# FFN weight blocks W1 and W3 in transfers of 256 rows, with another order of the products

## Chip, core and metric

One NeuronCore of a Trainium2 chip runs the whole program. The metric is the device time of one execution in microseconds (us), the median of several. The engines are PE (TensorE: `MATMUL`, with its weight loads shown as PEld), DVE (VectorE), ACT (ScalarE), POOL (GpSimd) and SP (SyncE), which here only issues transfers.

## What is computed

Two layers with shared weights, each a recurrent attention over 64 segments of 32 tokens with 8 memory tokens, and then a gated FFN. `x` is 2048 x 576, there are 32 heads of 128, and the FFN is 4608 wide; all inputs are bf16.

```
def _A_ref(x, mem0, Wq, Wk, Wv, Wo, seg_len):
    mem = mem0
    for s in range(n_seg):
        h = concatenate([mem, x[segment s]])                 # 8 + 32 tokens
        q, k, v = h@Wq, h@Wk, h@Wv                           # 32 heads of 128
        p = softmax(where(mask, q k^T * scale, -1e9))
        o = (p v) @ Wo
        mem = o[:8];  outs.append(o[8:])
def _B_ref(x, w1, w3, w2):
    return (silu(x@w1) * (x@w3)) @ w2
x = x + A(layernorm(x));  x = x + B(layernorm(x))            # layer 0
x = x + A(layernorm(x));  x = x + B(layernorm(x))            # layer 1
```

The memory makes each segment wait for the one before it, so PE is filled with several things at once.

## The kernel before

**Tiling.** 72 steps are run: in step t layer 0 works on segment t and layer 1 on segment t - 8, so that for most steps 2 x 40 query columns go through PE together. Attention weights stay in SBUF (tiles W, WV, WO). The FFN runs once per four steps as a "job" over 128 tokens of each layer, in 18 pairs of 128 hidden columns. For each pair the weights are fetched anew from HBM: `load_w13` brings 576 rows x 256 columns of W1 and of W3 into one of two buffers of tile W13, and `load_w2` brings 256 x 576 of W2 into one of two buffers of tile W2C. All of these transfers are issued by SP, one behind the other, and each waits there until PE has read the old content of its place. One pair's loads are, before the change, two transfers of 512 rows (256 KB), two of the last 64 rows (32 KB, the "tails"), and one of 288 KB for W2. In the profile tile W13 appears as `W`, like the attention weights.

**Completion marks.** SP's transfers use eight semaphores in turn, so a transfer also waits, before it is issued, until the one eight places ahead of it has landed.

**The order of products.** `make_nodes` builds a graph of nodes: a node is a group of matmuls (some 1 to 2 us), an evacuation, a step of the softmax, or a load. `plan` (line 76) places them. PE's order isn't searched there: it is read from the strings FIRST, FOUR and LAST (lines 199 to 222), one letter per node, joined as `ORDER = FIRST + FOUR * 11 + LAST`. FIRST has 805 letters, FOUR 224 (four steps and one FFN job, run eleven times), LAST 684. The other engines' nodes are put by `plan` at the first place where their inputs, buffers and engine are free by its own cost figures, and the program is recorded in that order. The letters are:

```
Q, q  products for q and k (32 full matmuls; 8 of the last 64 rows)     S  scores     T  transpose of p
P     p v         O, o  output product (32; 8)                           V, v, X, x, G, g  products for v
F, f  FFN up (16 full; 4 of the last 64 rows)   W, w  FFN down of the two layers   n, p, a, b, m  transposes
```

The string decides how far a product stands behind the ones it depends on: S waits for the evacuated q and k of its group (QKT), T for the softmax (SME, STAT, PB), P for the evacuated transposes (PTS), O for the evacuated P (OT), W for HTT.

**Forms of a product.** A node may run on the whole 128 x 128 array ("full"), in two column halves ("col", which issues each matmul as two with 64 columns of weights), in two row halves ("row", for contractions over 64 rows), or in quarters. `settle` in `plan` lets a node that may be full or col keep the form of its neighbours, so the string also decides how many matmuls are issued and how often the form changes.

**Step 0.** Its two V products, for tokens (VX) and for memory (VM), are issued as one sequence by `v_run` (line 871) when the second of them comes up in the order, whichever that is.

The lines of the profile: L591 is every matmul and weight load, L594 every ACT instruction, L597 every DVE instruction, L600 every transfer that SP issues, L1010 the clearing of PB on POOL.

Of the kernel before, what the change touches and what calls it, by code (L numbers as in the profile page):

```python
# [13 lines left out]
P = 128  # L14
# [30 lines left out]
class Slot:  # L45


    def __init__(self, pool, users=1):
        self.pool, self.users, self.i, self.end, self.begun = pool, users, None, 0.0, False
# [144 lines left out]
def ewh(*ns):  # L194
# [2 lines left out]


FIRST = (
    "amqqQQQQqSQqqQqSqqQSQTSvxVXPTPTOPTOPooOOooQQqqqqQSQvqqSVQQqTqSQPQOSToPXTOPTxoPOOooQqqqQQSVvqQQSQqqqQSqTQPOSTPTOP"  # L200
    "OToooPaOoQQqqqqQQSvSVQqqqQQQSqTPSXTOPTOPoTxoPOOooQQpQqqqvVqSnQQSFfqFQqfqqQTQSPFTfSOFPWOToPFToffPOOooWQqqqqQQSQQS"
    "FFfqfVvqTQWQqSFxffqQFPSXTWfPFTOPOTOPFOooooWQfqqqQQSFqfqVvQQSFfqTQPWQSqqfFTQOSfoPFTOPWFTOPooffOoFQqqQqqvSQQWSVqqf"
    "FQQWqqSTQPQSTOPabOTXPooTOPxxOooXqqpQQQqqSQnVvfSFTQqqqQQPSFffqQFTOPoSWTFfPOOTFPWOooofQQqfqqFSQFqqfgQGWTQPQSfqFQQq"
    "fqFSWTGFSggfGPGTOPOTfgFaPOOooooWVvqqfQQFFQSqfqQWQSqqfFQTQQqfqSFPWTSFPOTfoOPFWTOPffFOoooWQQqqqqQSbQQQqgqSGSTGPQTq"
    "gqQPOggSGTGPOTOPoooOoQqqqpQVpSQnQvqqqQnQFSTffqFQQPqSwTFPSffOOWTFPFTOPWOoooowFffqqQQQWSfqqFQwQSFqfqgGTQQPWfqSTFFg"
    "gfqGQwPGTOoSPFgfOGTOPWOoooFqqfqQQQQvSwqVSFqqfQQWwTFPQfqfqFTQSwPWSfFOTFPWwOTffFPOOaooooWQQqqqqQwSbQGQgqqSQTQPQqqg"
    "SGTSGPGggTOPOTOPoooOo"
)
FOUR = (
    "QvqqpQQpQqqVSSnnQQFqfqfFQTQfqqWSFPwTFPSfOOTFPwTOPWOooooFffqqQQQQqqSWFSFffqgGQTQPQQgqqqGSwTFPGSfgfgFTGOPOWTOPwOoo"  # L210
    "ooFqqQQQQqfqVvSSwWFfqfqQQTFWQwQSFffqqFPWTOPSowTFPffOTOFPWwOoooFqqfqQQQWQSqqqaQSQQbQqgqSGTSGPgTGPOTggOPGTOPwOoooo"
)
LAST = (
    "QqqqpQQQSnpQQqqqVSvTSnQFffqPFOQqTwPoSWTFPffFTOOWPwOoooFFqfqQQQqqfSQQwQfqqFTSGSqfgQFPWQgfqGTSFPGFTfggOOPGTOPwWOoo"
    "ooFFqffqQQwQWQSqqVSvqqQQTFQPSfqqQwTOWSPFTFPofOTOPwOoooWFfqfqQQQQqfqSFwWvVSFTfqqQQPWQqqSvTQVSPOTbOPwOTooPoxOoXqQp"
    "pVvQqqqQSQQnqqSQnqQFTSfqQPFTSOPfTFOPwTOPWOooooFqfqfQQQSVqqqvQQQwSfqFWTFPSfqqQTQOPSFTwfFPOTOPWOooooFfqqQQQSqfxvVX"
    "qfFQwWTSQFQqqqfQPWSTwFPffqQFTWSOwFPffOFTOPwOooooWFvqfqQQQSWqqVQwSFfqqfQFTQQSqqWPQTPSOoTOPwOToobPxOoXqqqQQQpvSVqQ"
    "qQSnqQFfSTQFPqqfQOTSFfPwTOoofPFTOPFOfoowQqqQFSQfqqqQQSVvqqfQFTQFSfqPQOTowPSFTfxXPOTOPFOooowVvqqQQQSqqfQQSqqfQFST"
    "QQPwqqFTSOfPFTOfPwTOPfoooOoFQQqqqqQSQQSqqQVvSfTFPqQQwqfTSFPOTOFPTOPfoooOoFpwnfffFFwFwfffFFFwfffFFwFwfffFFFwfffFF"
    "wFwfffFFFfww"  # L220
)
ORDER = FIRST + FOUR * 11 + LAST
# [2 lines left out]
class Opt:  # L225

    qk, qkt, sc, tr, pv, wo, wog, vm = 0.0079, -0.0342, 0.0268, 0.1447, 0.0406, 0.2653, 0.0725, 0.1407
    vmt, vx, vxt, ff, fft, win, w2, gstep = -0.0231, 0.2313, 0.0843, 0.2124, -0.1839, 0.8 * (LAG - 4), 0.1943, 0.0624
    ustep, mode_pen, hor, wait, bulk, ff_split, last_win, tail_at = 0.0315, 0.1194, 0.0162, 0.141, 0.02, False, 2.5, -1.5

# [337 lines left out]
class Emitter:  # L568


    def __init__(self, nc, tc, T, aps, nseg):
        self.nc, self.tc, self.T, self.nseg = nc, tc, T, nseg
        self.a = aps
        self.last = {}
        self.order_dep = mybir.DependencyInfo(mybir.DependencyClass.NoSync, mybir.DependencyReason.SCHED_ONLY)
        self.tail_w, self.ys, self.mode, self.v0 = {}, {}, None, []


    def ch(self, eng, inst):
# [111 lines left out]
    def load_w13(self, pr, w13):  # L691
        def f(n):
            fa = pr * 2 * P
            W = self.T.W13[:, w13.i]
            for kind, wd in ((0, self.a.w1), (1, self.a.w3)):
                self.dma(W[:, 4 * kind:4 * kind + 4], wd[0:4 * P, fa:fa + 2 * P].rearrange("(c p) f -> p c f", p=P))
            for kind, wd in ((0, self.a.w1), (1, self.a.w3)):
                self.dma(W[kind * R64:(kind + 1) * R64, 8], wd[4 * P:D, fa:fa + 2 * P])
        return f
# [168 lines left out]

        return [(p0, m, row, 2 * q + r) for p0, _, q, m, row in strips]

    def v_run(self, t, b, strips, tail):

        if t or tail:
            self.v_mm(t, [(b, strips)], tail)
            return
        self.v0.append((b, strips))
        if len(self.v0) == 2:
            self.v_mm(t, self.v0, False)

    def vx(self, t, k, b, tail):  # L880
        return lambda n: self.v_run(t, b, self.vx_strips(t, k), tail)

    def vm(self, t, k, b, tail):
        return lambda n: self.v_run(t, b, self.vm_strips(t, k), tail)

    def v_ev(self, b, p0, width, row, blk):
        return lambda n: self.cp(n, self.T.V[row:row + width, blk, :], self.bk(b)[p0:p0 + width, :])
# [444 lines left out]
```

## Time and profile before

| | us |
|---|---|
| median of 3 runs | 2688.06 (2684.2 to 2690.27) |
| profiled execution, its own time | 2690.27 |
| its span, first to last instruction | 2688.5 |
| PE busy in the span | 2621.6 |
| DVE busy | 2113.0 |
| ACT busy | 1346.6 |
| SP waiting for PE before an issue, in total | 1849.0 |

PE is busy for 98% of the span. Busy time of PE is a union of overlapping matmuls, so it is the time in which PE always had at least one product under way. The granted clock is 0.995. The transfers move 322.08 MB, 478177 packets, at a mean of 120 GB/s.

### The profile page before, as it was taken

The page shows a single profiled execution, that of the slowest core. Times are in us where ns is not written, and L with a number is a line of the kernel's source. Part 1 is how long each engine was busy: PE and PEld are TensorE (multiplying, and loading weights), DVE is VectorE, ACT ScalarE, POOL GpSimd, SP SyncE. Part 2 cuts the span into 40 slices and gives each one's busy share as a digit, 9 for nine tenths or more (in the row PEclk, how much of TensorE's full clock was granted, in tenths as well). Part 3 has the DMA queues.
Part 4 walks back from the last instruction along what each step waited for, and adds up shares of the span by engine and source line. Part 5 has one row for each costly group of instructions (what it writes and reads, how often), then busy time and mean ns, then how long its engine had stood idle before and what let it go on. Part 6 is the DMA issues. An engine that isn't in the chain of part 4 may idle for free.

```text
span 2688.5 us, 136826 instructions
## 1 busy us (share of the span) xinstructions
PE 2621.6 (98%) x60872; PEld 2292.9 (85%) x60925; DVE 2113.0 (79%) x5486; ACT 1346.6 (50%) x3915; POOL 332.2 (12%) x400
## 2 busy tenths in 40 slices
PE   5999999999999999999999999999999999999998
PEld 4788888889888888988888888888888888888886
DVE  4788887887878778788877878787787878787876
ACT  2655554454545455454545445454544545554552
POOL 1111110110111011011101101110110111011110
PEclk9999999999999999999999999999999999999999
DMA  9064524344343334434233443424343342334467
GB/s 318 4 180 124 159 76 125 89 120 118 102 124 88 111 98 119 118 107 126 82 112 96 119 118 108 128 78 115 93 123 114 109 134 73 116 91 134 129 175 239
DMA packets 478177, 322.08 MB, mean 120 GB/s; under 512 B 26024, under 2 KB 467760, under 8 KB 476944
## 3 DMA queue, kind: packets, MB, share of 16 engines
q1 hardware_dynamic: 474048, 305.43, 38.7%
q8 instruction: 477, 7.82, 1.2%
q0 software_dynamic: 3024, 6.93, 0.9%
q10 hardware_dynamic: 512, 0.94, 0.2%
q14 instruction: 116, 0.95, 0.1%
HBM read 308.49 MB, written 2.36 MB: 116 GB/s over the span
## 4 chain that ended last, share of the span: by engine, by line
PE 90%; DVE 3%; DMA 3%; ACT 2%; issue 1%; SPq 1%; POOL 0%; ACTq 0%; DVEq 0%; POOLq 0%
PE bank L591 90%; ACT V L594 1%; DMA W<-in_B_w_dram 1%; SPq L600 1%; DMA W<-in_A_Wk_dram 1%; DVE V L597 1%; DVE STAT L597 1%; DVE SME L597 1%; DMA XN<-in_A_x_dram 0%; ACT SME L594 0%; DVE PTS L597 0%; DVE PB L597 0%; ACT PTS L594 0%; DVE HTT L597 0%; DMA W2C<-in_B_w_dram 0%
## 5 line engine op out<-in xcount | busy, mean ns | idle before, releaser
L591 PEld LDWEIGHTS <-W 128*128 128x128 bf16 (+2 forms) x32064 | 1267.6, 100 | 124.9 <-issue 60.0
L591 PE MATMUL bank<-HT,W 128*128 128x80 bf16 (+3 forms) x23040 | 807.6, 197 | 18.7 <-issue 5.8
L591 PE MATMUL bank<-XTB,W 128*64 128x256 bf16 (+5 forms) x9024 | 664.4, 263 | 6.3 <-DMA W<-in_B_w_dram 3.7
L594 ACT ACTIVATE QKT<-bank 128x256 bf16<-128x256 f32 (+2 forms) x1477 | 343.6, 314 | 365.5 <-PE bank L591 337.5
L1010 POOL MEMSET PB<- 128x1024 bf16 x288 | 273.9, 951 | 1888.2 <-PE bank L591 1531.3
L591 PE MATMUL bank<-OT,WO 128*128 128x80 bf16 (+3 forms) x11520 | 409.7, 198 | 4.9 <-issue 3.4
L591 PEld LDWEIGHTS <-WO 128*128 128x128 bf16 (+1 forms) x11520 | 380.7, 102 | 30.4 <-issue 18.4
L594 ACT ACTIVATE V<-bank 32x512 bf16<-32x512 f32 (+1 forms) x594 | 335.8, 585 | 110.7 <-PE bank L591 104.4
L591 PE MATMUL bank<-WV,HT 128*32 128x512 bf16 (+4 forms) x3628 | 366.8, 384 | 4.5 <-issue 2.2
L591 PE MATMUL bank<-W2C,HTT 128*64 128x288 bf16 (+1 forms) x3040 | 320.5, 287 | 2.1 <-DMA W2C<-in_B_w_dram 1.4
L597 DVE TENSOR_REDUCE STAT<-SME 104x8 f32<-104x320 f32 (+1 forms) x576 | 274.5, 477 | 17.7 <-ACT SME L594 11.9
L597 DVE TENSOR_TENSOR PB<-SME,STAT 40x128 bf16<-40x128 f32 (+4 forms) x912 | 275.5, 336 | 10.8
L594 ACT ACTIVATE HTT<-bank 128x512 bf16<-128x512 f32 (+1 forms) x324 | 177.6, 557 | 200.4 <-PE bank L591 199.1
L591 PEld LDWEIGHTS <-HT 128*32 128x32 bf16 (+4 forms) x3680 | 158.0, 100 | 119.6 <-issue 17.7
L591 PEld LDWEIGHTS <-HTT 128*64 128x64 bf16 (+1 forms) x3104 | 229.9, 104 | 34.0 <-issue 2.1
L597 DVE SCALAR_TENSOR_TENSOR XR<-bank,XR 128x288 f32<-128x288 f32 x576 | 239.6, 446 | 17.2 <-PE bank L591 14.5
L597 DVE CAST QKT<-bank 128x128 bf16<-128x128 f32 (+4 forms) x571 | 154.6, 316 | 124.6 <-PE bank L591 123.5
L597 DVE SCALAR_TENSOR_TENSOR HTT<-HTT,bank 128x512 bf16<-128x512 bf16 (+1 forms) x324 | 202.0, 623 | 56.6 <-ACT HTT L594 52.4
L594 ACT ACTIVATE OT<-bank 128x320 bf16<-128x320 f32 (+1 forms) x425 | 157.0, 405 | 168.9 <-PE bank L591 165.1
L597 DVE TENSOR_TENSOR HTT<-HTT,bank 128x512 bf16<-128x512 bf16 (+1 forms) x324 | 203.5, 628 | 28.3 <-PE bank L591 0.5
L594 ACT ACTIVATE PTS<-bank 128x320 bf16<-128x320 f32 (+1 forms) x394 | 148.1, 405 | 131.6 <-PE bank L591 93.7
L594 ACT ACTIVATE SME<-SME 104x320 f32<-104x320 f32 (+1 forms) x288 | 135.4, 470 | 151.6 <-DVE SME L597 149.1
(61 smaller groups left out, 1836.2 us busy)
## 6 DMA issues: line engine op xcount, KB each, us to landing
W<-in_B_w_dram SPq DMA_DIRECT2D x612, 256.0 KB, 3.7
W2C<-in_B_w_dram SPq DMA_DIRECT2D x306, 288.0 KB, 3.3
W<-in_B_w_dram SPq DMA_DIRECT2D x612, 32.0 KB, 3.3
W<-in_B_w_dram SPq DMA_DIRECT2D x8, 1024.0 KB, 12.0
W<-in_A_Wq_dram SPq DMA_DIRECT2D x9, 512.0 KB, 9.1
WO<-in_A_Wo_dram SPq DMA_DIRECT2D x4, 1152.0 KB, 16.8
XR<-in_A_x_dram POOLq DMA_DIRECT2D x16, 288.0 KB, 3.5
WV<-in_B_w_dram SPq DMA_DIRECT2D x4, 1152.0 KB, 11.3
```

The source lines that it names most:

```text
L591: self.ch("PE", self.nc.tensor.matmul(out, lhsT=lhsT, rhs=rhs, start=start, stop=stop, skip_group_check=True, **k))
L594: self.ch("ACT", self.nc.scalar.activation(*a, **k))
L597: self.ch("DVE", getattr(self.nc.vector, fn_)(*a, **k))
L600: self.ch("SP", self.nc.sync.dma_start(out=out, in_=in_))
L1010: return lambda n: self.ch("POOL", self.nc.gpsimd.memset(self.T.PB[:, pb.i], 0.0))
```

## The change

Two things differ. In `load_w13` the 512 rows of W1 and of W3 are fetched in two transfers of 256 rows each (128 KB) instead of one of 512 rows, so a pair's loads are seven transfers and not five; their bytes and the layout in SBUF are the same, and the tails, W2 and the bulk loads of the last FFN job (`tail_load`) are untouched. And the strings FIRST, FOUR and LAST are others, with the same letters in the same numbers. With them goes a detail of step 0: VX is now put by, and both V products are issued when VM comes up.

```diff
 FIRST = (
-    "amqqQQQQqSQqqQqSqqQSQTSvxVXPTPTOPTOPooOOooQQqqqqQSQvqqSVQQqTqSQPQOSToPXTOPTxoPOOooQqqqQQSVvqQQSQqqqQSqTQPOSTPTOP"
+    "amQQQQqqqqSSqqQQQTSqqQSqxXVvPTPTOPOOTooPoOoQQqqqvSVqQQQSqQqqQSTxqPQTSOPXoTOPTaPOOoooQQqqqqQSQQSQqqqVSTvQQqXPTSPTO"
...
 FOUR = (
-    "QvqqpQQpQqqVSSnnQQFqfqfFQTQfqqWSFPwTFPSfOOTFPwTOPWOooooFffqqQQQQqqSWFSFffqgGQTQPQQgqqqGSwTFPGSfgfgFTGOPOWTOPwOoo"
-    "ooFqqQQQQqfqVvSSwWFfqfqQQTFWQwQSFffqqFPWTOPSowTFPffOTOFPWwOoooFqqfqQQQWQSqqqaQSQQbQqgqSGTSGPgTGPOTggOPGTOPwOoooo"
+    "QqqvpQQpQqqVSSnnQQFffqqFQTqqfSFPwTWFSffOPFTWPOTOPwOooooFqfqqQQQWQqwSSFFffgqGQTQPQQgqqqGTwSQPWGSFTfgfgFPGOTOPOwOo"
+    "oooFqffqQFQWQqSVvqQQQqqqfFTWPwSSFFqffqQQTOwSWPFTffFOPWTwPOOooooFqqfqQQQWQSqqqaQSQQbQqgqSGTSGPgTGPOTggGPOTOPwOoooo"
 )
 LAST = (
...
@@ load_w13
             for kind, wd in ((0, self.a.w1), (1, self.a.w3)):
-                self.dma(W[:, 4 * kind:4 * kind + 4], wd[0:4 * P, fa:fa + 2 * P].rearrange("(c p) f -> p c f", p=P))
+                for c in (0, 2):
+                    self.dma(W[:, 4 * kind + c:4 * kind + c + 2], wd[c * P:(c + 2) * P, fa:fa + 2 * P].rearrange("(c p) f -> p c f", p=P))
             for kind, wd in ((0, self.a.w1), (1, self.a.w3)):
                 self.dma(W[kind * R64:(kind + 1) * R64, 8], wd[4 * P:D, fa:fa + 2 * P])
@@ step 0
-    def v_run(self, t, b, strips, tail):
-
-        if t or tail:
-            self.v_mm(t, [(b, strips)], tail)
-            return
-        self.v0.append((b, strips))
-        if len(self.v0) == 2:
-            self.v_mm(t, self.v0, False)
-
     def vx(self, t, k, b, tail):
-        return lambda n: self.v_run(t, b, self.vx_strips(t, k), tail)
+        def f(n):
+            if t == 0 and not tail:
+                self.x0 = (b, self.vx_strips(t, k))
+                return
+            self.v_mm(t, [(b, self.vx_strips(t, k))], tail)
+        return f
 
     def vm(self, t, k, b, tail):
-        return lambda n: self.v_run(t, b, self.vm_strips(t, k), tail)
+        return lambda n: self.v_mm(t, ([self.x0] if t == 0 and not tail else []) + [(b, self.vm_strips(t, k))], tail)
```

More of the change, by code (lines that the diff above doesn't have):

```diff
@@ L199 @@
 FIRST = (
-    "amqqQQQQqSQqqQqSqqQSQTSvxVXPTPTOPTOPooOOooQQqqqqQSQvqqSVQQqTqSQPQOSToPXTOPTxoPOOooQqqqQQSVvqQQSQqqqQSqTQPOSTPTOP"
[L201 to L204, printed above, removed]
@@ L205 @@
-    "gqQPOggSGTGPOTOPoooOoQqqqpQVpSQnQvqqqQnQFSTffqFQQPqSwTFPSffOOWTFPFTOPWOoooowFffqqQQQWSfqqFQwQSFqfqgGTQQPWfqSTFFg"
-    "gfqGQwPGTOoSPFgfOGTOPWOoooFqqfqQQQQvSwqVSFqqfQQWwTFPQfqfqFTQSwPWSfFOTFPWwOTffFPOOaooooWQQqqqqQwSbQGQgqqSQTQPQqqg"
-    "SGTSGPGggTOPOTOPoooOo"
+    "amQQQQqqqqSSqqQQQTSQqqSxXVvPTPTOPOOTooPoOoQQqqqvSVqQQQSqQqqQSTxqPQTSOPXoTOPTaPOOoooQQqqqqQSQQSQqqqVSTvQQqXPTSPTO"
+    "POOToooPOoxQQqqqQSVqvQQqSqQTQPSqqQOTSoPOTPTOPooOoQQpqqqQvSVQnqQFSqfqQQTSfqqFPQFTSOfoPWTOFPfTOPFOoooWQqqfQQSQFfqq"
@@ new lines @@
+    "vVfSFTWQFqqfQPQFSqqfQTXPSWTFOfPOTxOPFOooooWQQqqqfQSFqfqVvQWTQSFfqPQQSfqqFTQOSfPFTOaFPWTOPooofOoFQqqfQQSWqqfQFSvV"
+    "TQqqQWPQSQTPOqqOboSoTXPXTPOOooxxQQpQqqqVqQnvSSFqfQqQFfQTSfqqFPQTOPSWTFFPffOTOPWOooooFQQqfqqQQqfSWFGSqqgQTQFPQgqf"
+    "SGTFqfQOoSPWFfggGTGPOaTWPOOoooFQQvqfqVSFqqfQQQqqfSFQTQFqfqSQWPFfSTOPFTWPOffooOTFPWOooFQqfqqQQWSQQqQqSqqbQSTGggqQ"
+    "PGTOSPGTggOPGTOPoooOoQqqqpQpQQqvVSSnnQFqfqqQQTFPqffSQOTWPFOSTwFPffFTOWPwOooooFqqffQQFQqqwWSFqqfQQQwWSTSGqgfFPQFf"
+    "qgTGQPGTfgSWFgPGTOOPOOwooooFqqfQQQWQffqqFwFSSVvFQfqqQQTQWqqSwPFaSTffFPOTOWPwfTFPOOooooWQQqqqqQSbQQQSqqGTQgqqSQPG"
@@ L208 @@
+    "TgggSGPGTOPOTOPwOoooo"
 )
 FOUR = (
-    "QvqqpQQpQqqVSSnnQQFqfqfFQTQfqqWSFPwTFPSfOOTFPwTOPWOooooFffqqQQQQqqSWFSFffqgGQTQPQQgqqqGSwTFPGSfgfgFTGOPOWTOPwOoo"
-    "ooFqqQQQQqfqVvSSwWFfqfqQQTFWQwQSFffqqFPWTOPSowTFPffOTOFPWwOoooFqqfqQQQWQSqqqaQSQQbQqgqSGTSGPgTGPOTggOPGTOPwOoooo"
+    "QqqvpQQpQqqVSSnnQQFffqqFQTQqqfSFPwTWFSffOPFTWPOTOPwOooooFqfqqQQQWQqwSSFFffgqGQTQPQgqqqGTwSQPWGSFTfgfgFPGOTOPOwOo"
+    "oooFqffqQFQWQqSVvQQQqqqfFTWPwSSFFqffqQQTOwSWPFTffFOPWTwPOOooooFqqfqQQQWQSqqqaQSQQbQgqqSGTSGPgTGPOTggGPOTOPwOoooo"
@@ L212 @@
 )
 LAST = (
[L214 to L218, printed above, removed]
@@ L219 @@
-    "QQPwqqFTSOfPFTOfPwTOPfoooOoFQQqqqqQSQQSqqQVvSfTFPqQQwqfTSFPOTOFPTOPfoooOoFpwnfffFFwFwfffFFFwfffFFwFwfffFFFwfffFF"
+    "QqqqpQQpQSqqqQQnVvSnSQTFqfqfQPFTOFPoSTwFfPOTOPWOoooFqffqQQQQqqfSFWSGwqqgQQTQPFgqffFTGWwPFSgffqFQWGSwTFPGTgfOPOOO"
+    "ooooWFqqfqQQQSwQqqqVSvQTQFPQqSfqfFTQWwPSOTFffPOTOPFOWoooowQQqfqFSQwQWFqqfVSTvWQQqqPQQqqSTOSoPVvwTOPbTOPooxOoXqqQ"
+    "QpvQqqSVpQQqqQSTQPqqQSnnOFffToSFPTOPFTOPWOooowQfqfqFQQSvqqVQFSfqqQQwTSWPQFTffqqQOPSWTFPFTOwPOOooooXfqxFQQQqfqfqF"
+    "SQwVvSWQFTQqqfqQWPQSTwqffFPOFSWTOPwFffTOPFOWooowoFqqfQQQSFQqfqvVSTQqqfQWwPSFTqqQPQWSTOPOOooowbTxPOoXqqQQQpSQqvqV"
@@ L220 @@
+    "qSnQQFffqFQqqSQTPSTFfPOwOToFPofTOPFOoowQfqqfQFSQVvqqqQQSFQfqqqQSQTwPSFTFPffXTOOPxTOPwOooooFQfqqVvQQQSqfqFSQQfqqq"
+    "FQTSQPwqOTSFPofTFPOOTPwOoooQfqqqQQSwFQqfqvSVqTQQqPQSQqTSfOPFOTfooPFTOPOooFpwnfffFFwFwfffFFFwfffFFwFwfffFFFwfffFF"
     "wFwfffFFFfww"
@@ L575, in __init__ @@
         self.order_dep = mybir.DependencyInfo(mybir.DependencyClass.NoSync, mybir.DependencyReason.SCHED_ONLY)
-        self.tail_w, self.ys, self.mode, self.v0 = {}, {}, None, []
+        self.tail_w, self.ys, self.mode = {}, {}, None
     def ch(self, eng, inst):
```

## The prediction

> **What bounds the kernel now.** I read the engine totals first, then the busy time by stretches cut where FIRST, the eleven repeats of FOUR, and LAST begin (the first matmul of the repeats starts at 530.4 us, of LAST at 2251.1), then the waits, then SP's queue.
>
> ```profile
> PE 2621.6 (98%) x60872; PEld 2292.9 (85%) x60925; DVE 2113.0 (79%) x5486; ACT 1346.6 (50%) x3915; POOL 332.2 (12%) x400
> ```
>
> ```profile
> 13.00:80.00 67.00, 48.76 (x1237) 36.93 (x1238) 35.78 (x102) 24.60 (x69) 7.89 (x9) 0.92 0.75 278
> 80.00:530.40 450.40, 439.72 (x11295) 382.36 (x11297) 362.04 (x969) 239.25 (x721) 61.88 (x71) 0.99 0.40 113
> ...
> 530.40:2251.10 1720.70, 1711.61 (x38153) 1511.28 (x38196) 1376.53 (x3555) 870.99 (x2508) 203.96 (x242) 1.00 0.38 109
> 2251.10:2640.00 388.90, 383.23 (x9628) 330.81 (x9628) 301.96 (x779) 202.62 (x594) 51.47 (x58) 1.00 0.46 133
> 2640.00:2688.50 48.50, 38.23 (x582) 31.47 (x574) 28.85 (x71) 9.18 (x24) 1.13 (x2) 0.94 0.72 234
> ```
>
> After the stretch come its length and PE's busy time. PE's idle time is 10.7 us in the body of FIRST, 9.1 in all eleven repeats (0.8 in each of 156.4 us), 5.7 in LAST up to 2640, and 10.3 in the last 48.5 us, where the bulk loads of the last FFN set the pace. So between 80 and 2640 us the kernel is PE's own pace plus 25.5 us. A change can act on the pace (how many matmuls, how many changes of form) or on that idle time.
>
> ```profile
> W<-in_B_w_dram SPq DMA_DIRECT2D x612, 256.0 KB, 3.7
> W2C<-in_B_w_dram SPq DMA_DIRECT2D x306, 288.0 KB, 3.3
> W<-in_B_w_dram SPq DMA_DIRECT2D x612, 32.0 KB, 3.3
> ```
>
> ```profile
> SPq L600 <- PE bank L591: 1849.0, 738, 76.9
> ...
> PEld L591 <- DMA W<-in_B_w_dram: 4.2, 2, 2.6
> PE bank L591 <- DMA W<-in_B_w_dram: 3.7, 2, 2.5
> ```
>
> The transfers: SP waits for PE, 1849 us in all, and PE hardly ever waits for an FFN block (7.9 us in the whole span, 5 of them in the last 30 us). The loads are hidden, with SP idle for two thirds of the time.
>
> **The change part by part.** Everything is added to the profiled execution, 2690.27 us (span 2688.5 and 1.8 around it); that run is 2.2 us above the median of the three, so the forecast for a median is the sum less 2.2.
>
> *Matmuls issued.* The built program has 60995 matmuls and weight loads against 60925. The 70 more come from nodes that take the col form: T 89 against 68 of 288, P 62 against 79, F 166 against 159, others about even. The price of a form is read from the order of time:
>
> ```profile
> 1373.15 0.46 PE L591 MATMUL bank<-ident,PB 104*64 104x80 bf16 x15
> 1373.43 0.28 PE L591 MATMUL bank<-XTB,W 128*64 128x256 bf16 x1
> ...
> 1386.17 0.45 PE L591 MATMUL bank<-ident,PB 104*128 104x80 bf16 x8
> 1386.45 1.32 PE L591 MATMUL bank<-OT,WO 128*128 128x80 bf16 x32
> ```
>
> From the start of a T to the start of what follows: 0.28 us full (1386.17 to 1386.45), about 0.33 col (1373.15 to the second group of 31 F at 1373.48). So T costs 21 x 0.05 = +1.0, P gives back 17 x 0.05 = -0.8, and F is about even (16 full ones 110 ns apart, 1.76; 32 half ones in 1.70). Sum +0.5 with the rest; bounds -1 and +3.9 (70 halves at the 55 ns apart that the half F show).
>
> *Changes of form.* Counted along the order of the nodes there are 1092 now and 1110 after: 3 more in FIRST, 2 more in each FOUR (57 against 55), 7 fewer in LAST. The price:
>
> ```profile
> 1367.07 2.46 PE L591 MATMUL bank<-HT,W 128*128 128x80 bf16 x64
> 1369.46 0.39 PE L591 MATMUL bank<-WV,HT 64*128 64x512 bf16 x2
> ```
>
> 64 full products of 80 columns at 36 ns (the median distance of their starts over the whole trace) are 2.30 us; to the first row product it is 2.39. The median distance before a change is 131 to 134 ns for 80 columns, so a change costs 0.096 us, and 18 cost +1.7. Bounds: 0 (all under a wait) and +3.6 (double, as some changes after 256 columns stand 205 ns apart and not 110).
>
> *Waits of products for ACT and DVE.* The strings move nearly every node. For both I laid the mean start-to-start time of each kind of node in this trace end to end and asked, for each product, how much PE work stands between it and the product whose evacuated result it reads. Where that is less than the path by ACT or DVE, the shortfall is counted: 0.9 us for T to P and P to O (an evacuation of 0.44 to 0.49, the 0.2 us of a matmul, and hand-overs), 1.0 for Q to S, 4.5 for S to T (the rows add 485, max 479, subtract 492, exp 471, sum 479, reciprocal 203, two or three PB of 283 to 350 ns, and hand-overs), 1.5 for O to the next step. Shortfalls in LAST: before T to P 1.8, P to O 2.2, Q to S 0.9, O to Q 0.9, sum 5.7 (PE's measured idle there is 5.7); after 2.8, 3.5, 1.9, 1.1 and 0.1, sum 9.4. So +3.6. In the repeats: 12.0 before (mostly F to W 4.2 and O to v 7.0; measured idle 9.1), 9.3 after (all O to Q); scaled by 9.1/12.0, -2.0. In FIRST 21.5 before (measured 10.7 past 80 us), 26 after; scaled by a half, +2.3. Sum +3.9. This counts no queueing on DVE, which is 79% busy; bounds -9 (all idle time of the repeats goes) and +8.
>
> *The loads.* 612 transfers of 256 KB become 1224 of 128 KB. The issues stand 0.55 us apart where nothing is waited for (1067 such pairs in the trace), so SP gets 612 x 0.55 = 336 us more work, against 1849 us in which it waits for PE: hidden by that wait. Not hidden is the place in the queue: the tails and W2 of a pair are issued two places, 1.1 us, later, and when two pairs' buffers come free together, 2.2 us. Behind a late tail stands f, and with it PE and all. In this trace a tail lands a median 6.5 us before its f, and 17 of 596 land less than 1.1 us before. The eighth transfer back had landed more than 1.2 us before its successor's issue in 99% of cases, so with seven per pair the eight marks seldom bind. What the new strings leave: PE work between the last reading of a W13 buffer and the first use of its new content is under 6 us for 18 loads before (4.4 us at the least) and for 47 after (4.7 at the least), 33 of these being three in each repeat at 4.9 to 5.0. A load that is issued all at once needs 4 x 0.55 until its first tail and then 3.1 (the median of the tails in the repeats) to land: 5.4. One of the three, where the tails' buffer isn't freed earlier than the rest, is short by 0.4, that is 11 x 0.4 = 4.4. I take half of this, +2. Bounds: 0, and 33 x 1.1 = 36.
>
> The finer release (the first 256 rows may be refetched when PE has read them) is worth two matmuls, 0.22 us, once per load and under SP's wait: nothing. [...]
>
> *The start.* V's detail in step 0 issues the same products; the start waits for the attention weights, in the same order of loads: 0, bounds -2 and +3 (the new string begins with four Q, which need the large blocks, and the old one with two q, which need the small ones).
>
> Sum: 0.5 + 1.7 + 3.9 + 2 = +8.1. 2690.3 + 8.1 - 2.2 = 2696.
>
> **The rivals.**
> - *The loads become a wait.* All three tight loads of each repeat are late, each by 0.5 us: 33 x 0.5 = 16.5, and with the order's 6.1 it is 2688 + 22.6 = 2711. For it: 47 tight loads and not 18, and issues of 1.4 us now and then (2% of the transfers). Against it: tails and blocks come free at different moments.
> - *No difference.* Shortfalls are absorbed by neighbouring waits and the changes of form fall under them: 2688 + 0.5 to 2, 2689. For it: the pace per product is the same and both strings hold the same letters. Against it: LAST's shortfall, which matches the measured idle time for the old string.
> - *Faster.* The eleven repeats lose their idle time: the new FOUR has no F to W shortfall and all that is left is O to Q, which is an overlap with the memory's evacuation. If that is covered, 9.1 us go, less the 2.1 of 22 changes of form at 0.096: 2688 - 7 = 2681, where LAST's 3.6 is absorbed as under "no difference" (2685 where it isn't). It decides from the point where a repeat takes less than 155.9 us.
> - *The change does nothing to the transfers.* Same packets, same bytes, issued in the same queue: this is the 0 of the loads' term, 2694, and part of the forecast.
>
> **How the numbers follow.** Forecast (order +6, loads 0 to +4; 2691 to 2702) 0.56; loads as a wait 0.14; no difference 0.20; faster 0.10. A measurement of this kernel tells 0.2%, 5.4 us, from no change: under 2682.7 is faster, over 2693.4 slower. Slower: the loads' 0.14 and 0.50 of the forecast's 0.56, 0.64. Same: 0.20 and the forecast's rest, 0.06, 0.26. Faster 0.10. The likeliest case's own range is 2691 to 2702; down to 2683 it takes in "no difference" and the weaker half of "faster", up to 2713 the loads.
>
> **What would show it.** In the profile after: a repeat of FOUR at 156.4 to 157.2 us, PE's idle time in it about as now; LAST (now 431.6 from 2251.1 to its last product) at 435 to 439, with its P and O products waiting for PTS and OT; 1224 transfers of 128 KB landing in about 3 us; PE's waits for FFN blocks once per repeat or never. The forecast is wrong if repeats are a microsecond or more longer with waits on W (the loads), or if they are shorter than 156 us.

## The result, and the profile after

The changed kernel takes 2702.67 us (median of four runs, 2700.21 to 2705.93) against 2687.72 for the kernel before beside it: a ratio of 1.0057, interval 1.0040 to 1.0075, some 15 us more. The forecast was 2696, the range 2683 to 2713. The profiled execution took 2702.87 us, its span is 2701.1.

The engine totals of the kernel after, and its busy time by the same stretches as before (the repeats of FOUR now start at 532.0 us, LAST at 2257.6; after each stretch its length and PE's busy time):

```profile
PE 2627.6 (97%) x60931; PEld 2287.6 (85%) x60995; DVE 2103.0 (78%) x5463; ACT 1362.1 (50%) x3938; POOL 332.3 (12%) x400
```

```profile
80.00:532.00 452.00, 440.55 (x11200) 380.37 (x11203) 350.55 (x943) 242.20 (x736) 61.21 (x70) 0.99 0.40 112
532.00:2257.60 1725.60, 1712.55 (x38316) 1505.83 (x38370) 1370.60 (x3544) 883.94 (x2519) 203.95 (x242) 1.00 0.38 109
2257.60:2646.50 388.90, 376.73 (x9317) 323.71 (x9318) 302.56 (x775) 195.75 (x572) 48.88 (x56) 1.00 0.45 130
2646.50:2701.10 54.60, 46.29 (x804) 39.68 (x804) 33.85 (x86) 12.66 (x35) 3.44 (x5) 0.91 0.68 225
```

PE's idle time is 11.4 us in the body of FIRST (10.7 before), 13.0 in the repeats (9.1), 12.2 in LAST up to the bulk loads (5.7) and 8.3 behind that (10.3). PE's busy time grew by 6.0 us, 1 of it in the repeats; part of that is a lower granted clock, 0.992 against 0.995 (told at the end). The transfers (bytes, median us from issue to landing) and the waits (line waited for: total us, times, longest):

```profile
W<-in_B_w_dram SPq DMA_DIRECT2D x1232, 128.0 KB, 2.9
W2C<-in_B_w_dram SPq DMA_DIRECT2D x306, 288.0 KB, 3.3
W<-in_B_w_dram SPq DMA_DIRECT2D x612, 32.0 KB, 2.9
```

```profile
SPq L600 <- PE bank L591: 1677.1, 1028, 73.6
...
PEld L591 <- DMA W<-in_B_w_dram: 13.1, 26, 1.6
PE bank L591 <- DMA W<-in_B_w_dram: 6.3, 9, 1.4
PE bank L591 <- DMA W2C<-in_B_w_dram: 5.1, 7, 1.1
```

A half lands sooner than a whole (2.9 against 3.7 us) and a tail sooner than before (2.9 against 3.3), and yet PE now waits 26 times for a W block where it had waited twice. (The weight load and the matmul behind it are often stopped by one late block, as at 1186.33 us below, where they idle 1.65 and 1.37 us, so the totals of PEld and PE are not to be added.) Between 80 and 2640 us PE itself stops for 4.6 us at tails (7 times), for 3.6 us at W2 (5 times), which stands behind the tails in SP's queue, and for 0.3 us at a block; before, those stops were 0.2 us in all. A transfer's own time got better; when it is issued got worse. One such place in full, in the fifth repeat, the longest of all (158.1 us). First when SP issued the loads of one pair and two loads of W2, how long it was at each issue, and when each landed (us, read out of the trace):

```
issue     at SP   landed after   what
1179.39   0.37    2.41           W1, 256 rows
1179.87   0.93    2.83           W1, 256 rows
1180.89   0.42    -              W3, 256 rows
1181.40   0.43    2.29           W3, 256 rows
1181.88   0.47    2.29           tail of W1
1182.40   0.59    3.88           tail of W3   -> 1186.28
1183.09   0.54    3.91           W2
1183.72   1.83    4.37           W2
```

Then the timeline of that stretch (start, duration, engine, line, operation, count, and in brackets the idle time and what ended it):

```profile
1184.10 0.43 PE L591 MATMUL bank<-QKT 128*40 128x40 bf16 x16
1184.46 0.22 PEld L591 LDWEIGHTS <-W 64*128 64x128 bf16 x5
1184.47 0.50 PE L591 MATMUL bank<-XTB,W 64*128 64x256 bf16 x5
...
1186.33 0.11 PEld L591 LDWEIGHTS <-W 64*128 64x128 bf16 x3 [1.65 <-DMA W<-in_B_w_dram]
1186.33 0.39 PE L591 MATMUL bank<-XTB,W 64*128 64x256 bf16 x3 [1.37 <-DMA W<-in_B_w_dram]
```

Two f stand here, eight matmuls in all; five run, and the sixth, the second matmul of the second f, needs the tail of W3. That was the sixth of its pair in SP's queue, 3.0 us behind the first, with one issue of 0.93 us ahead of it, and took 3.88 to land where 2.9 is the median. PE resumes 0.05 us after it lands.

The same phases in the four profiles that matter most, from PE's first matmul of each (the last two are told of below; "start" is the time of that matmul):

| us | start | FIRST | eleven repeats | LAST to the end | span |
|---|---|---|---|---|---|
| before | 13.4 | 517.0 | 1720.6 | 437.4 | 2688.5 |
| after | 13.5 | 518.5 | 1725.6 | 443.5 | 2701.1 |
| old order, no loads | 12.6 | 509.1 | 1720.0 | 436.2 | 2678.0 |
| new order, no loads | 12.8 | 507.6 | 1720.6 | 440.8 | 2681.9 |

So repeats and LAST lost 5 and 6 us. FIRST varies by several us between executions of one string (with 512 rows the old one takes 515.4 to 519.9 us in three profiles, the new one 510.6 and 513.6 in two), so a single profile doesn't settle its share.

### The profile page after: what moved, and what is told of

Its sections match the earlier page's. It is cut to its first block, busy times and chain, and to the rows that moved or that the text cites. A ratio compares the mean times of both kernels' runs of the same rounds, so it can differ in the third digit from the quotient of the medians.

```text
span 2701.1 us, 138237 instructions
## 1 busy us (share of the span) xinstructions
PE 2627.6 (97%) x60931; PEld 2287.6 (85%) x60995; DVE 2103.0 (78%) x5463; ACT 1362.1 (50%) x3938; POOL 332.3 (12%) x400
## 3 DMA queue, kind: packets, MB, share of 16 engines
q8 instruction: 477, 7.82, 1.2%
## 4 chain that ended last, share of the span: by engine, by line
PE 84%; DVE 6%; DMA 4%; ACT 3%; issue 1%; SPq 1%; POOL 0%; ACTq 0%; DVEq 0%
PE bank L591 84%; DMA W<-in_B_w_dram 2%; ACT V L594 1%; DVE STAT L597 1%; DVE HTT L597 1%; SPq L600 1%; DVE PB L597 1%; DVE SME L597 1%; DMA W<-in_A_Wk_dram 1%; DVE V L597 1%; DMA XN<-in_A_x_dram 1%; DMA WO<-in_A_Wo_dram 0%; DVE LNS L597 0%; DMA W2C<-in_B_w_dram 0%; ACT PTS L594 0%
## 5 line engine op out<-in xcount | busy, mean ns | idle before, releaser
L594 ACT ACTIVATE QKT<-bank 128x64 bf16<-128x64 f32 (+2 forms) x1500 | 349.6, 312 | 353.6 <-PE bank L591 348.0
L594 ACT ACTIVATE V<-bank 64x512 bf16<-64x512 f32 (+1 forms) x606 | 343.0, 585 | 95.0 <-PE bank L591 86.3
L597 DVE SCALAR_TENSOR_TENSOR XR<-bank,XR 128x288 f32<-128x288 f32 x576 | 245.6, 445 | 27.2 <-PE bank L591 22.8
L591 PEld LDWEIGHTS <-HT 128*32 128x32 bf16 (+5 forms) x3584 | 154.5, 99 | 126.0 <-issue 19.0
L591 PEld LDWEIGHTS <-HTT 128*64 128x64 bf16 (+1 forms) x3136 | 224.0, 105 | 39.7 <-issue 6.8
L597 DVE CAST QKT<-bank 128x128 bf16<-128x128 f32 (+4 forms) x548 | 147.5, 316 | 84.4 <-PE bank L591 82.0
## 6 DMA issues: line engine op xcount, KB each, us to landing
WV<-in_B_w_dram SPq DMA_DIRECT2D x4, 1152.0 KB, 12.2
```

The costliest lines, as they stand in the source:

```text
L591: self.ch("PE", self.nc.tensor.matmul(out, lhsT=lhsT, rhs=rhs, start=start, stop=stop, skip_group_check=True, **k))
L594: self.ch("ACT", self.nc.scalar.activation(*a, **k))
L597: self.ch("DVE", getattr(self.nc.vector, fn_)(*a, **k))
```

## The experiments

Ratios are to the kernel before, run beside each on the same chip (one chip for e1 to e4, another for e5 to e12), with 95% intervals; 0.1% is 2.7 us.

| kernel | order | rows per transfer | ratio | interval |
|---|---|---|---|---|
| after | new | 256 | 1.0057 | 1.0040 to 1.0075 |
| e1 | old | 256 | 1.0018 | 1.0009 to 1.0027 |
| e2 | new | 512 | 1.0024 | 1.0015 to 1.0032 |
| e3 | only LAST new | 512 | 1.0015 | 1.0006 to 1.0024 |
| e4 | only FOUR new | 512 | 1.0023 | 1.0014 to 1.0032 |
| e5 | new | 512, tails first | 1.0056 | 1.0044 to 1.0068 |
| e6 | new | 256, tails first | 1.0113 | 1.0098 to 1.0128 |
| e7 | old | 512, tails first | 1.0038 | 1.0023 to 1.0052 |
| e8 | old | 128 | 1.0845 | 1.0831 to 1.0859 |
| e9 | old | none | 0.9974 | 0.9965 to 0.9983 |
| e10 | new | none | 0.9991 | 0.9982 to 1.0000 |
| e11 | only FIRST new | 512 | 0.9993 | 0.9984 to 1.0002 |
| e12 | old | 512, W2 by POOL | 1.0039 | 1.0027 to 1.0052 |

**The two halves of the change, each alone.** e1 has the new `load_w13` and the old strings with the old step 0:

```diff
-                self.dma(W[:, 4 * kind:4 * kind + 4], wd[0:4 * P, fa:fa + 2 * P].rearrange("(c p) f -> p c f", p=P))
+                for c in range(0, 4, 2):
+                    self.dma(W[:, 4 * kind + c:4 * kind + c + 2], wd[c * P:(c + 2) * P, fa:fa + 2 * P].rearrange("(c p) f -> p c f", p=P))
```

> The kernel before with W1 and W3 in transfers of 256 rows and its own order of products. My theory (the order costs about 6 us, the late tails 2 to 4 and both add up): the old order leaves more room behind a load, so +1 to +4 us, ratio 1.000 to 1.0015. Rival 'loads': the two more places in SP's queue are most of the 15 us, so +9 or more, ratio 1.003 to 1.006. Rival 'order alone': 0, ratio 1.000.

e2 has the new strings and the old `load_w13`. Its code of step 0 is the old one too, but X stands ahead of V in the new FIRST, so it issues both V products when VM comes up, as the change does (strings not printed):

```diff
-FIRST, FOUR, LAST = ...        # the strings before
+FIRST, FOUR, LAST = ...        # the strings after
```

> The kernel before with the new strings and transfers of 512 rows as before. My theory: about +6 to +10 us, ratio 1.002 to 1.004, most of it in LAST, and PE's waits for FFN blocks as rare as in the kernel before. Rival 'loads': 0 to +3 us, ratio 1.000 to 1.001. Rival 'order alone': +15 us, ratio 1.0055.

Both are slower, +0.18% (4.8 us) and +0.24% (6.5 us). Their sum, 0.42%, is less than the 0.57% of both, by 4 us, which is about what the intervals allow. The waits for W blocks in e1:

```profile
PEld L591 <- DMA W<-in_B_w_dram: 10.9, 13, 3.6
...
PE bank L591 <- DMA W<-in_B_w_dram: 7.8, 6, 3.4
```

The transfers alone, at the old order, make 13 waits out of 2.

**LAST alone, FOUR alone.** e3 and e4 each take one string from the change and leave the rest as before:

```diff
-LAST = ...                     # e3: the string before; e4: FOUR in its place
+LAST = ...                     # e3: the string after
```

> The kernel before with the new LAST alone (FIRST and FOUR old, 512 rows). My theory: +3 us (shortfalls +3.6, seven changes of form fewer -0.7), ratio 1.001. Rival (the whole cost of the order is in LAST): the same ratio as with all three new strings, +6 or more.

> The kernel before with the new FOUR alone in its eleven repeats (512 rows). My theory: 0 to +1 us (22 changes of form more +2.1, shortfalls -2.0), ratio 1.000. Rival (the repeats carry the cost): 11 x 0.45 = +5 us, ratio 1.002, each repeat 0.45 us longer, as in the changed kernel; where the changed kernel's repeats are longer only by loads, this one's stay at 156.4.

+0.15% and +0.23%. In e4's trace the eleven repeats are 1723.5 us, 2.9 more than before, and this stands at one place of the string, the two f products in "FPwTWFSffO": without a wait they take 0.54 us, and in five of the eleven repeats longer, 3.2 us in all. (Without loads, in e10 below, they take 0.54 us in all eleven.) There the tails land about when their f comes: in one repeat 0.1 us ahead of the end of the S before (no wait), in another, issued at the same point of the string, 1.0 us behind that end (a wait of 0.9). If each of the 224 nodes of a repeat is given its shortest distance to the next over the eleven repeats, the sums are 156.07 us for the old FOUR and 155.9 to 156.0 for the new one: undisturbed, the new string is no slower. (Such a sum of shortest distances is less than any real repeat.)

**Tails ahead of their blocks.** If a late tail is the trouble, the tails can be issued first:

```diff
-            for kind, wd in ((0, self.a.w1), (1, self.a.w3)):
-                self.dma(W[:, 4 * kind:4 * kind + 4], ...)
             for kind, wd in ((0, self.a.w1), (1, self.a.w3)):
                 self.dma(W[kind * R64:(kind + 1) * R64, 8], ...)
+            for kind, wd in ((0, self.a.w1), (1, self.a.w3)):
+                self.dma(W[:, 4 * kind:4 * kind + 4], ...)
```

> The new strings with transfers of 512 rows, and the two tails of a pair issued ahead of its two blocks. My theory now (the new FOUR isn't slower by itself: its undisturbed repeat is 156.0 us, and it loses where two f products stand behind a tail that lands within 0.1 us of them): the wait at these two f goes, repeats at 156.0 to 156.2 without the 0.3 to 0.9 us that some have, and the order's ratio falls from 1.0024 to 1.0005 to 1.0012 (LAST's part stays). Rival (the order costs by its changes of form and its waits for ACT and DVE, as I predicted): the ratio stays at 1.0024.

> The changed kernel (new strings, 256 rows) with the two tails of a pair issued ahead of its four halves. My theory: most of the 15 us is late tails, so the ratio to the kernel before falls from 1.0057 to about 1.002 (LAST's 3 us and halves that are now the last to land). Rival (not the tails' place but the number of issues, or the order's forms): it stays at 1.005 or more.

> The kernel before with the tails ahead of the blocks, as a control of the edit by itself. My theory: the old order leaves its tails more room, so there is little to win: ratio 0.9995 to 1.0005. Rival (tails first helps or hurts whatever the order, for instance as a block waits behind a tail whose place isn't free yet): 2 us or more, either way.

A miss: all three are slower than the same kernel with tails last, by 0.32%, 0.56% and 0.38% (e5 against e2 by ratios from two chips); for e6 and e7 the rival's number came. The wait at "FPwTWFSffO" is gone in e5, where the two f take 0.54 us in all eleven repeats, but 4.7 and 2.7 us of waits stand at a q and a Q of the same repeats instead. No FFN block is late there. The profile puts these waits to DVE, and DVE's layer norm had waited for its input XN, which SP issues in the same queue. DVE's waits for XN in e2 and then in e5:

```profile
DVE LNS L597 <- DMA XN<-in_A_x_dram: 3.1, 4, 2.4
```

```profile
DVE LNS L597 <- DMA XN<-in_A_x_dram: 22.5, 13, 2.9
```

And the longest of the stops, in e5:

```profile
1517.15 0.82 DVE L597 BATCH_NORM_STATS2 LNS<-XN 128x6 f32<-128x288 bf16 x2 [2.89 <-DMA XN<-in_A_x_dram]
...
1521.97 0.40 DVE L597 SCALAR_TENSOR_TENSOR XR<-bank,XR 128x288 f32<-128x288 f32 x1
1522.43 0.30 PE L591 MATMUL bank<-HT,W 64*128 64x80 bf16 x7 [1.38 <-DVE XR L597]
```

Between these rows DVE works without a break, so the 2.89 us reach PE's bank. In the repeats XN lands 19.6 to 21.5 us after the start of the two f, and 17.8 to 19.6 in e2: it is issued behind the two blocks now and not behind the two tails. Moving a load forward in SP's queue moved another back, one that isn't the FFN's. In e6 DVE waits 23.4 us for XN (6.5 after the change). The traces don't show where e7's 10 us lie: its span is only 3.0 us longer than before's.

**Transfers of 128 rows.** Four for each of W1 and W3, eleven loads per pair, at the old order:

```diff
-                self.dma(W[:, 4 * kind:4 * kind + 4], wd[0:4 * P, fa:fa + 2 * P].rearrange("(c p) f -> p c f", p=P))
+                for c in range(0, 4, 1):
+                    self.dma(W[:, 4 * kind + c:4 * kind + c + 1], wd[c * P:(c + 1) * P, fa:fa + 2 * P].rearrange("(c p) f -> p c f", p=P))
```

> The kernel before with W1 and W3 in four transfers of 128 rows each: eleven transfers per pair and not seven or five. By the place in the queue alone (0.55 us an issue) a tail is 3.3 us later than before and not 1.1, so about three times the 5.2 us of 256 rows, +15 us or somewhat more, ratio 1.006 to 1.01. By the eight completion marks (a pair now needs more than eight, so its last transfers wait until its own first have landed, some 3 us): +100 us or more, ratio 1.04 and up, and SP waiting for transfers of B_w. Rival (halving the transfers costs nothing by itself): the ratio stays at 1.0018.

+8.45%, 228 us. Transfers and waits of e8:

```profile
W<-in_B_w_dram SPq DMA_DIRECT2D x2448, 64.0 KB, 2.1
```

```profile
PEld L591 <- DMA W<-in_B_w_dram: 137.7, 137, 7.6
...
PE bank L591 <- DMA W<-in_B_w_dram: 108.0, 111, 7.5
PE bank L591 <- DMA W2C<-in_B_w_dram: 43.3, 53, 2.7
```

A block of 64 KB lands in 2.1 us, the quickest of all, and PE waits the longest. The number is what the eight completion marks were expected to cost, but they are not the cause: between 80 and 2600 us SP waits 2.2 us in all for an earlier load of the FFN to land (2.4 before, 1.5 after). What grew is SP's time at issues: after the first 80 us 836 us before, 1154 after, 1724 here. Eleven issues 0.5 to 0.55 us apart are some 6 us, where a repeat has 8.7 us for a pair (156.4 / 18) and the issues can't start until PE has read the old content. That would make the cost grow faster than the count of issues, as it does: two more per pair cost 4.8 us, six more 228. No run changed the issue time alone, so this part is argued from the trace. And not all of it is waiting: of the 218 us by which the profiled span is longer, PE is idle in 137, and its busy time for the same matmuls is 81 longer (2702.5 against 2621.6), at a granted clock of 0.975 against 0.995.

**No loads.** To tell what the order costs by itself from what it costs through the loads, the FFN's blocks are fetched only the first time for each buffer (the bulk loads for the last FFN stay):

```diff
         def f(n):
             fa = pr * 2 * P
             W = self.T.W13[:, w13.i]
+            if (13, w13.i) in self.had:
+                return
+            self.had.add((13, w13.i))
...
         def f(n):
             fa = pr * 2 * P
+            if (2, w2.i) in self.had:
+                return
+            self.had.add((2, w2.i))
```

> The order before, with the FFN's blocks of W1, W3 and W2 fetched only the first time for each buffer: all later loads of the FFN's 306 pairs are left out (the FFN works with weights of other columns), the bulk loads of the last FFN stay. SP then has almost nothing in its queue in the repeats. Theory (the order costs time only through the room it leaves for the loads): the undisturbed repeat is 156.07 us, against 156.4 measured, and the late loads of FIRST and LAST go too, so 3 to 10 us less than the kernel before, ratio 0.996 to 0.999. Rival (PE's idle time is waits for ACT and DVE, as the prediction had it): 1.000.

> The new order, with the same loads left out as in the run with the order before. Theory (the order costs time only through the loads): its undisturbed repeat is 155.9 to 156.0 us, 0.1 shorter than that of the order before, so it is equal to that run or up to 5 us faster: the difference between the two is -0.2% to 0.05%. Rival (forms, changes of form and shortfalls against ACT and DVE, as the prediction summed them): it stays 6 us, 0.23%, slower than the order before without loads, as it was with loads of 512 rows (0.24%).

My theory fell in half. The order before without loads is 0.26% faster than with them: "hidden" loads cost 7 us even there. But the new order stays slower without any load: 2683.68 against 2679.70 us, eleven runs of each on one chip, nine of e9's under all of e10's; ratio 1.0015, interval 1.0011 to 1.0019 by resampling the runs, 4.0 us. By the table of phases it is LAST: +4.6, with +0.6 in the repeats and -1.5 in FIRST. The stretches of LAST up to 2600 us, e9 and then e10:

```profile
2241.70:2600.00 358.30, 356.94 (x8882) 307.75 (x8879) 284.26 (x728) 188.89 (x553) 47.31 (x54) 1.00 0.02 6
```

```profile
2241.00:2600.00 359.00, 353.49 (x8671) 303.92 (x8669) 284.55 (x726) 184.40 (x534) 45.37 (x52) 1.00 0.02 6
```

PE is idle for 1.4 us in the one and 5.5 in the other. (The windows end at the same time and not at the same product: x8882 against x8671. Up to the same product, the transposes of the last FFN job, LAST takes 395.8 us in e9 and 401.0 in e10; PE's waits there for ACT and DVE are 0.8 and 5.7 us.) The waits of PE in that stretch of e10, of which e9 has only some of 0.2 to 0.4 us:

```profile
PE bank L592 <- DVE V L598: 0.9, 1, 0.9
PE bank L592 <- DVE PB L598: 0.8, 2, 0.5
PE bank L592 <- ACT QKT L595: 0.8, 2, 0.4
PE bank L592 <- DVE XR L598: 0.6, 1, 0.6
...
PE bank L592 <- ACT OT L595: 0.5, 1, 0.5
```

Products stand closer behind the evacuations that they read than these take: the mechanism that the prediction had for LAST, though not all its places. Of the 5.7 us, 2.9 are at PTS, OT, QKT and HT, which it had counted, and 2.3 at V, PB and XR, which it had at nothing. A repeat is 156.38 us in e9 and 156.40 in most of e10's: FOUR's order costs next to nothing by itself.

**FIRST alone.** e11 takes FIRST from the change, nothing else (step 0 as in e2).

```diff
-FIRST = ...                    # the string before
+FIRST = ...                    # the string after
```

> Only FIRST (with its detail of step 0) is new, FOUR and LAST and the transfers of 512 rows are those before. Theory (the parts add: LAST alone +0.15%, FOUR alone +0.23%, all three +0.24%): FIRST is worth -0.14%, some 3.8 us faster, ratio 0.9985, of it at the start of the string. Rival (the parts don't add; all three share one loss): 1.000. The prediction had FIRST at +2.6 us, 1.001.

0.9993, 0.9984 to 1.0002: both 0.9985 and 1.0000 lie inside, so it is not told apart; that FIRST costs 0.1% is excluded. e10's FIRST, 1.5 us shorter than e9's, speaks for a small gain.

**One issue fewer in SP's queue.** If the number of issues in SP's queue is what costs, a kernel with four per pair should gain:

```diff
-        return lambda n: self.dma(self.T.W2C[:, w2.i], ...)
+        return lambda n: self.swdma(self.T.W2C[:, w2.i], ...)
```

> The kernel before, with the 306 loads of W2 issued by POOL and not by SP, so that SP issues four transfers per pair and not five; bytes, order and places are the same. Theory (what costs is the number of issues that stand one behind the other in SP's queue): the next pair's first blocks are 0.55 us earlier behind W2, SP's issue time falls by some 170 us, and the late loads of before get fewer: ratio 0.998 to 1.000. Rival (POOL issues behind its clearing of PB, which waits for PE and ACT, and itself takes longer to issue): W2 comes later, PE waits for W2C in place of W: 1.001 to 1.01.

The rival came: +0.39%. Its transfers of W2, and what PE waits for:

```profile
W2C<-in_B_w_dram POOLq DMA_DIRECT2D x306, 288.0 KB, 3.7
```

```profile
PE bank L591 <- DMA W2C<-in_B_w_dram: 8.6, 10, 2.4
...
PEld L591 <- DMA W<-in_B_w_dram: 1.5, 3, 0.9
PE bank L591 <- DMA W<-in_B_w_dram: 1.1, 2, 0.7
```

PE's waits for W fell (4.2 and 3.7 us before), as the theory had it, and its waits for W2 rose from 1.4 to 8.6: POOL clears PB in its own order and holds W2 behind that. At one such stop POOL waited 5.58 us for PE ahead of clearing PB and issued two loads of W2 right behind it (1341.60 us, 0.7 us each), the second took 6.2 us to land, and PE went on 0.04 us later. The theory's half is seen, the gain isn't. No version here that computes the whole result is shown to beat the kernel before.

## Why the prediction was right in direction and short in size

Its sum was +8.1 us on the profiled execution; measured are 15. The range was wide enough to hold that. The order's part comes out near its size partly by luck, as its terms miss in opposite ways.

- **The order, +6.1 predicted.** Measured without loads: +4.0 us (e10 against e9). *LAST's waits, +3.6*: PE's idle time there rose by 4.1 us with waits for V, PB, QKT and OT, and LAST is 4.6 longer without loads; half of the waits are at places that the term didn't count. It was set at 435 to 439 us up to its last product and is 438.0 after (431.5 before), but that includes late loads and clock. *FOUR*: -2.0 of waits and +2.1 of changes of form gave nothing, measured +0.6 in eleven repeats. The two terms can't be told apart. *FIRST, +2.3*: wrong; e10 and e11 show none of it, rather 1.5 to 2 less. Half of a shortfall that was worked out on paper was no better than a guess. *Matmuls and forms, +0.5 and +1.7*: PE's busy time is 2621.8 in e9 and 2623.7 in e10, +1.9 against 2.2. That is the same size, but it tests neither term: busy time also moved with the granted clock (2618.4 in e2, with the same new order, at 0.996 against 0.993 in e10).
- **The loads, +2 predicted: the mis-sized term.** Of the 15.3 us (1.0057) 4 are the order's own, so some 11 came by the loads: e1 shows 4.8 at the old order, e2 less the order's own 4.0 shows 2.5 that the new order loses with 512 rows, and about 4 appear only with both, near the edge of what the intervals resolve. The mechanism was the one named: the tails and W2 issued 1.1 us later, f (and W) behind them; PE's stops at them are 8.2 us between 80 and 2640 us. Four things in the working made it small. It costed one of three tight loads per repeat, and none in FIRST and LAST, though most of the loss is there: against e2, which has the same order with 512 rows, the profile after is 1.2 us longer in the repeats, 7.9 in FIRST and 3.9 in LAST. It went by the first tail, four issues back (4 x 0.55 + 3.1 is 5.3, not the 5.4 given), where an f needs both: with five issues the sum is 5.85, 0.9 more than the 4.9 to 5.0 that the tight loads have, and the stop shown above is at the second tail. It used medians, 0.55 us per issue and 3.1 to land, where a late load is made by the tail of the distribution: after the first 80 us, 197 of SP's 2163 issues take over 0.7 us (132 of 1555 before), up to 1.8 in the stretch shown above, and one tail in ten takes 3.8 us or more. And it took PE's waits for FFN blocks as all that loads cost before. Its 7.9 us for them adds PEld's 4.2 and PE's 3.7, which are the same two stops; PE's own are 5.2 us with W2, 4.9 of them under the bulk loads. Taking the other loads away gave 7 us, where the profile had named 0.2.
- **"Hidden by SP's wait of 1849 us".** This was the choice that failed. SP's wait fell to 1677.1 and was still 62% of the span; a queue with that much idle time is late all the same, because SP's idle time lies before a place is free and the issues come after it. e8 shows how steep this gets.
- **What would show it.** Ten of eleven repeats lie between 156.38 and 157.22 us (156.4 to 157.2 was written), one is 158.11; the mean is 0.45 us longer than before, and the sign that was to prove the forecast wrong, a microsecond or more per repeat, came in one. "Once per repeat or never" nearly holds: W blocks stop 15 weight loads in eleven repeats. 1224 halves landing in about 3 us: 2.9.
- **The rivals.** "The loads become a wait", 2711, was too much: not all three tight loads of each repeat are late, and not each time. "No difference" and "faster" are excluded by the interval; their ground, that FOUR isn't slower by itself, is right, but LAST and the loads decide. "The change does nothing to the transfers" fell with e1. The likeliest case's own range ended at 2702, the median is 2702.67; the whole range holds it.
- **The size of a transfer.** At one order 512, 256 and 128 rows cost 0, +0.18% and +8.45%, while the blocks landed in 3.7, 3.1 and 2.1 us at the median (before, e1, e8); with the new order halves took 2.9. So single transfers gained, 0.6 to 0.8 us by halving 256 KB, and the loss comes from when they are issued.

## What to carry to other kernels

Before splitting transfers, count the issues that stand ahead of the last one needed, and set that time against the stretch from "place free" to "first use", not against the queue's total idle time. Cost it with the slow issues and landings of the trace rather than their medians, and at every use, because one late block stops PE and what stands behind it (1.37 us at the tail shown above). Look at all that the queue carries: here the layer norm's input stood in it too. A version with the loads taken out tells what the hidden ones cost and what an order costs by itself, which no trace of the whole kernel did.

## What had not been expected

**Half the clock behind some stops of PE.** The traces list the granted clock: it is whole or half, and half mostly for 3.4 or 6.8 us. Past the first 80 us, in the profiles before and after and in e9 and e10, each half-clock stretch up to PE's last product begins during a stop of PE (of 0.3 us or more) or within 2 us behind one (before four stretches, 0.5 to 0.9 us behind; after four, 0 to 1.8); many stops are followed by none (there are 36 such stops before and 51 after). Two stretches of e10 by `--windows` (the third number from the end is the clock), and the same groups of products in each:

```profile
2596.00:2600.00 4.00, 4.00 (x109) 3.51 (x105) 3.90 (x12) 1.93 (x8) 1.25 (x2) 1.00 0.02 4
2624.00:2630.00 6.00, 5.75 (x117) 5.35 (x118) 3.27 (x10) 2.51 (x9) 0.95 (x1) 0.50 1.06 325
```

```profile
2597.93 0.97 PE L592 MATMUL bank<-OT,WO 128*128 128x40 bf16 x32
2599.33 1.07 PE L592 MATMUL bank<-XTB,W 128*128 128x128 bf16 x16
...
2626.54 1.25 PE L592 MATMUL bank<-OT,WO 128*128 128x40 bf16 x32
2627.88 1.88 PE L592 MATMUL bank<-XTB,W 128*128 128x128 bf16 x16
```

Up to PE's last product and past the first 80 us the half clock was granted for 13.7 us before and 20.5 after. Set against the same products at the whole clock in the same trace, it costs an estimated 5.1 and 7.3 us, so some 2 of the 15 us, and 52 us in e8. In e9 and e10 it costs 6.9 and 6.4 us and doesn't explain the difference between them.

**What looks like PE waiting for its own code.** Of PE's stalls over 0.5 us past the first 80 us, 6 of 11 carry no releaser in the profile before ("issue"). One from e9, where no FFN block is fetched but the bulk loads run:

```profile
2626.15 0.23 PE L592 MATMUL bank<-PTS,V 128*128 128x40 bf16 x3
2628.62 3.95 SPq L601 DMA_DIRECT2D WV<-in_B_w_dram  x2
2629.69 0.28 PE L592 MATMUL bank<-PTS,V 128*128 128x40 bf16 x5 [3.31 <-issue]
```

It stops within one group of eight like matmuls, for 3.3 us. The queues of the kernel before list what could be late (packets, MB, share of the engines):

```profile
q8 instruction: 477, 7.82, 1.2%
```

7.82 MB over 477 packets is 16 KB each, and, if all of it is PE's, 64 bytes for each of the 121850 matmuls and weight loads. The packet nearest to the stall above landed at 2628.15, 1.54 us before PE went on; the two other long ones of e9 end 1.55 and 1.49 us after a packet. Over the fourteen profiles 66 of the 67 such stalls that the profile puts down to nothing end 1.1 to 1.75 us after a packet landed; packets come every 5.6 us, so chance would put some 12% there. They make 6.6 us before, 4.7 after and at most 10.2, so they don't carry the difference. Without the FFN's loads they are gone from FIRST (3.1 us before) and make 8.8 us in e9 under the bulk loads. That these packets are PE's code, and that the loads make some of them late, is inferred from the queue's kind, its bytes and where the stalls lie; no run moved the code alone.

**Landing times spread.** Between identical repeats the same tail, issued at the same point, lands up to 2 us apart. After the change blocks of 128 KB land in 2.8 us at the median between 80 and 2600 us, in 4.2 or more for one in ten and 5.2 or more for one in a hundred. So one place of FOUR costs nothing in some repeats and 1.6 us in another (nothing in any repeat of e10, without loads).
